# A block-recurrent attention and a serf layer on one core: the first batch's list of steps rewritten, with half of the state loads later

## The chip, the core and the metric

One of the eight cores of a Trainium2 chip runs the whole kernel. The time is the device time of one execution in microseconds (us), and the median of three runs is given. A core has TensorE (PE; its weight loads are PEld in the profile), VectorE (DVE), ScalarE (ACT), GpSimd (POOL) and SyncE (SP). They run side by side, each in the order of its own instructions, and wait for each other by semaphores. SP issues nearly all the DMAs here, and it too works in order: a DMA whose condition is not met holds up all that stand behind it.

## The reference

Inputs are x (8 batches, 8 heads, 512 tokens, 64 wide), state (8, 8, 32, 64), both float32, and the weights w_in (512 x 2048) and w_out (2048 x 512), which come as 64-bit floats and are worked on as float32.

```python
scores = scale * np.matmul(x, state.transpose(0, 1, 3, 2))
scores = scores - scores.max(-1, keepdims=True)
a = np.exp(scores)
a /= a.sum(-1, keepdims=True) + 1e-09
xread = np.matmul(a, state)
# the same with x and state exchanged gives sread; both are joined:
# 8 * (512 + 32) = 4352 rows of 8 heads * 64 = 512 numbers
h = x @ w_in
sp = np.maximum(h, 0.0) + np.log1p(np.exp(-np.abs(h)))   # softplus
g = h * erf(sp)
return (g @ w_out).astype(np.float32)
```

## The kernel before

**Batches.** Batch 0 is computed by a list of named steps written out by hand (`order0`), and batches 1 to 7 by a loop that comes after it (two halves of the hidden width a batch, seven products where a plain scheme needs eight). The 256 state rows come last. The change is in the list and in one load ahead of it. The last 40 steps of the list are open to the loop's order, so list and loop meet without a gap.

**How the list works.** Every step has a name in the table `do`; the names are run through in the order in which they stand, and `in_order` fixes that order on PE, DVE, ACT and SP. Since each step issues on one engine, the list is four queues in one: only the order among the steps of one engine counts. A number ahead of a name (`3*tm1`) sets `leads[0]`, and the step begins with so many matmuls of the identity with itself (`lead`, line 192), which compute nothing that is used. They run as soon as their PSUM buffer is free, ahead of the step's own inputs.

**The steps of batch 0**, with the engine and the line in the profile:

- `x0` to `x3`: PE turns two heads of x each (L780); `x0_v` and so on: the copy out of PSUM. A last letter `_a` puts a copy on ACT (L756) and `_v` on DVE (L757).
- `st`: PE turns the state of batch 0 (L796). `s0`, `s1`: scores of four heads each (L807). `tm0`, `tm1`: the scores turned (L815).
- `max`, `less`, `sum`, `inv`, `norm` on DVE and `exp` on ACT: the softmax over states for either group of heads. `ta0`, `ta1`: its result turned (L826), copied by `ta0_` and `ta1_` into `aT`. `to0`, `to1` hold only fill.
- `m00` to `m32`: PE mixes the state with a part of w_in (L908): first digit the group of 512 hidden columns (0 to 3), second digit the part. `m00x` and `m00y` are halves. `m020_a` and the like are copies. With it xread needs no product of its own: `h01` is `aT` by mixed part (L919), a 128 x 512 block of h of group 0.
- `soft` and `erf` on ACT (L952; L954, or L957 for two blocks), `mul` on DVE (L959). Softplus, erf and exp each need a table that ACT loads before (ACT_TABLE_LOAD).
- `p021`: group 0, output row block 2, hidden block 1: g times w_out (L926), summed in one of four PSUM banks `o0` to `o3`.
- `big`, `wt`, `wz`, `wn`, `tw`, `read`: the other softmax, over tokens, and sread.
- `u0`, `u1`: PE turns the states of batches 1 to 7 (`turn_states`, L893) in the banks `o2` and `o3`, and `u0_v`, `u1_v` copy them back. A `p` step in bank o2 or o3 comes after that.
- `q` (scores), `n0`, `n1` (mixed parts), `qm` to `qr`, `cm`, `ca`: preparation of batch 1. `lxq1..`, `lxq2`, `lx1`: loads of x for batches 1 and 2. `kept` writes w_in to DRAM.

**Weights.** They come as 64-bit words in pieces of 1 MB, i0, i1, o0, o1, i2 and so on (i of w_in, o of w_out; group g uses i(2g), i(2g+1), o(2g), o(2g+1)). `fetch` (a `get` in the list) issues the next piece on SP (L156) into one of three `raw` buffers, and thus waits until DVE and ACT have done with the piece three before. ACT does `i2a0` and `i2a1` (L166, L168) and DVE `i2v0`, `i2v1`, `i2v2` (L171, L172, L173) to make float32 of it. Piece i0 is done in halves (`i0a0`, `i0+a0`).

**Ahead of the list**, SP issues its half of x, the state of batch 0, the pieces i0, i1 and o0, and then `load_st` (L125): eight DMAs, one for each head, of the states of batches 1 to 7.

Of the kernel before, what the change touches and what calls it, by code (L numbers as in the profile page):

```python
# [17 lines left out]
def kernel(  # L18
# [18 lines left out]
    B, H, S, D = x.shape  # L37
# [59 lines left out]
    def load_xq(b, hs=range(H)):  # L97
# [11 lines left out]
    st = const.tile([P, B, P], F32, name="st")  # L109
    away0 = ring[:, 1, 0].rearrange("p k i t -> p (k i t)")  # L110
    st0 = away0[:, 512:640].rearrange("p (g d) -> p g d", g=2)
    x0 = xin.tile([P, NC, H, D], F32, name="x").rearrange("p c h d -> p (c h d)").rearrange(
        "p (h c d) -> p h c d", h=H, c=NC)
# [5 lines left out]
        if i == 1:  # L119
            nc.sync.dma_start(out=st0, in_=state[0].rearrange("(g h) n d -> (h n) g d", g=2))  # L120

    def load_st():
        for h in range(H):
            i, e = h // 2, h % 2
            nc.sync.dma_start(out=st[Ns * i:Ns * i + Ns, 1:B, D * e:D * e + D],  # L125
                              in_=state[1:B, h].rearrange("b n d -> n b d"))
# [571 lines left out]
    def put_x(b, h):  # L698
        rows = out[TB * b:TB * b + S].rearrange("(p c) e -> c p e" if b == 0 else
                                                "(c p) e -> c p e", p=P)  # L700

        def go(r, ot, c=slice(0, d_model), more=False):
            if more:
                nc.gpsimd.dma_start(out=rows[2 * h + r][:, c], in_=ot[:, c], accum_op=ALU.add)  # L704
            else:
                nc.sync.dma_start(out=rows[2 * h + r][:, c], in_=ot[:, c])
        return go
# [35 lines left out]
    def fetch():  # L743
        if len(made) < len(pieces):
            kind, j = w = pieces[len(made)]
            made[w] = (weights_in if kind == "i" else weights_out)(j)
# [4 lines left out]
    def step(name, f, *args):  # L751
        do[name] = lambda: f(*args)

    def copied(name, out, in_):

        do[name + "a"] = lambda: nc.scalar.copy(out(), in_())  # L756
        do[name + "v"] = lambda: nc.vector.tensor_copy(out(), in_())  # L757
# [124 lines left out]
    def groups0():  # L882
# [47 lines left out]
        def put(r):  # L930
            ot = outs.tile([P, d_model], F32, name="ot", bufs=3)
            nc.scalar.copy(ot, acc[r])
            put_x(0, r // 2)(r % 2, ot)

        for k, bs in enumerate((slice(1, 5), slice(5, B))):
            step("u%d" % k, turn_states, k)
            copied("u%d_" % k, lambda bs=bs: st[:, bs, :], lambda k=k: ps_s[k])
# [106 lines left out]

    for _ in range(3):
        fetch()
    load_st()
    start0()
    groups0()
    weights0()  # L1050
    ready = next0()

    order0 = """
        first x0 x0_v x1 x1_a st st_v i0a0 x2 x2_v s0 x3 i0v0 s00_v i0a1 i0v1 i0v2 s01_a tm0 x3_a
        i0+a0 i0+v0 i0+a1 max0 s1 s10_a i0+v1 s11_a less0 exp0 m00x i1a1 3*tm1 i0+v2 max1 m00y
        m000_a sum0 m001_a get 6*to1 m01x less1 m01y exp1 lxq14 inv0 norm0 4*ta0 i1a0 sum1 inv1
        m010_v norm1 u0 o0a0 o0a1 ta1 m011_a ta1_a i1v0 ta0_v h000 i1v1 i1v2 h01 m02 o1a0 o1v0 o0v0
        h001 o1a1 u1 m021_v m020_v soft01 lxq11 o0v1 o0v2 u0_v get soft00 h03 erf00+ h02 soft02
        mul00 p020 p000 p010 u1_v soft03 p030 o1v1 mul01 p011 erf02+ big1 p031 p001 p021 big0 big
        wt1 o1v2 wt0 mul03 mul02 p012 i2a0 wz wn0 tw0 i2a1 p033 i2v0 i2v1 i2v2 get p022 p002 tw0_a  # L1060
        i3a0 i3v0 wn1 m10 m101_v i3a1 i3v1 p013 m100_a get o2a0 h11 i3v2 o2a1 h10 get m12 m121_v
        p023 o2v0 p032 lxq17 p003 soft11 get soft10 erf10+ m120_v h13 h12 o2v1 mul10 o2v2 mul11 o3a0
        o3a1 p110 i4a0 p120 p101 p130 soft13 lxq10 p121 p111 o3v0 o3v1 i4v0 o3v2 i4a1 i4v1 i4v2
        lxq13 soft12 erf12+ get get lxq12 p131 p100 mul13 mul12 i5a0 i5v0 i5a1 p123 m20 p113 m200_a
        p103 m201_a p122 i5v1 get h21 i5v2 m22 h20 o4a0 o4v0 o4a1 o4v1 m220_v o4v2 m221_v tw1 tw1_v
        soft21 h22 h23 lxq15 o5a0 lxq16 get get o5v0 p133 o5a1 p112 p132 o5v1 o5v2 get soft20 erf20
        mul20 soft23 p102 p220 soft22 erf22 xq1v mul22 i6a0 i6v0 erf23 mul23 p230 i6a1 read read_a
        i6v1 i6v2 p210 erf21 mul21 q q1_a qm1 qm3 p203 q0_a qm0 i7a1 qm6 p233 qm2 qm4 n1 n10_a p213
        n11_a i7a0 i7v0 p201 m30 p221 p223 m301_a i7v1 m300_a o6a1 n0 o6a0 n00_v h31 n01_a h30 get
        p200 o7a0 get o6v0 p212 soft31 soft30 p211 qm5 i7v2 m32 cm0 cm1 cm3 erf31 p232 erf30 qm7  # L1070
        o6v1 kept p222 m321_a m320_a h33 p231 lxq2 mul30 o6v2 p300 qm8 mul31 o7v0 o7a1 o7v1 qe0 qs0
        qe2 qe3 qe1 qs1 h32 soft32 erf32 p301 get qs2 qr0 qr2 ca0 soft33 get erf33 qr1 qr3 mul32
        o7v2 p320 ca1 ca3 p311 lx1 p202 p321 cm2 p331 mul33 ca2 p310 p330
    """
    steps0 = order0.split()
    for n, name in enumerate(steps0):
# [246 lines left out]
```

## Time and profile before

| | us |
|---|---|
| three runs | 718.74, 719.79, 720.80; median 719.79 |
| profiled execution | 718.98 |
| its span, from first to last instruction | 717.2 |
| PE busy | 707.9 |
| DVE, ACT busy | 541.1, 377.3 |
| first product of batch 1 on PE (the list's work on PE is over) | 109.18 |

A line of a timeline gives start and duration in us, engine, line of the source, operation, what it writes and reads, how many instructions are merged in it, and in brackets the idle time of the engine before it with what ended that. A line of waits gives who waited for whom, then us in all, how many times, and the longest. `x18` on PE counts two instructions for each float32 matmul. The granted TensorE clock is 1.0 through the span.

### The profile page before, as it was taken

Reading aid. Unit: us, or ns where it says so; the run is one execution under the profiler, and the core shown is the slowest. Engines: PE = TensorE matmul, PEld = TensorE weight load, DVE = VectorE, ACT = ScalarE, POOL = GpSimd, SP = SyncE. Lnnn points to the kernel's source line nnn. Section 1 sums busy time; section 2 is a strip of 40 time slices with the busy share of each in tenths; the row PEclk is TensorE's granted clock in tenths of the full one; section 3 lists DMA queues with packets and bytes.
Section 4 is the critical chain, followed back from the end, with each engine's and each line's share of the span. In section 5 each row is a group of like instructions: output and inputs, shape, how many; then the busy total and the mean of one; then the engine's idle time right before and its main releaser. Section 6 shows DMA issues by size and latency. Waiting matters only on the chain.

```text
span 717.2 us, 10922 instructions
## 1 busy us (share of the span) xinstructions
PE 707.9 (99%) x4273; PEld 560.0 (78%) x4273; DVE 541.1 (75%) x876; ACT 377.3 (53%) x537; POOL 25.2 (4%) x34
## 2 busy tenths in 40 slices
PE   8899999999999999999999999999999999999998
PEld 6344347688878878887888878887888888889997
DVE  5888898889868987798776967697877757664533
ACT  5899895647364525544455435462464535442340
POOL 0000000000100000000000000000000000000000
PEclk9999999999999999999999999999999999999999
DMA  8679786650348162513623280615142321102100
GB/s 268 191 215 276 235 225 189 141 169 30 49 95 211 27 134 46 160 36 92 96 30 146 60 148 1 176 31 149 28 114 75 93 43 24 35 30 30 21 11 29
DMA packets 144067, 74.64 MB, mean 104 GB/s; under 512 B 123024, under 2 KB 132624, under 8 KB 142480
## 3 DMA queue, kind: packets, MB, share of 16 engines
q1 hardware_dynamic: 139152, 65.89, 33.3%
q0 software_dynamic: 4032, 7.34, 7.7%
q8 instruction: 33, 0.54, 0.3%
q10 hardware_dynamic: 832, 0.72, 0.3%
q14 instruction: 18, 0.15, 0.1%
HBM read 49.81 MB, written 20.45 MB: 98 GB/s over the span
## 4 chain that ended last, share of the span: by engine, by line
PE 94%; DMA 3%; ACT 2%; DVE 0%; issue 0%; SPq 0%
PE o L641 48%; PE h L489 13%; PE at L489 10%; PE o L926 6%; PE h L534 3%; PE o L616 3%; DMA raw<-in_moe_w_out_dram 2%; PE h L383 2%; PE at L383 2%; PE h L919 1%; PE at L919 1%; PE at L275 1%; PE o L224 1%; DMA x<-in_x_dram 1%; PE at L908 1%; ACT L957 0%
## 5 line engine op out<-in xcount | busy, mean ns | idle before, releaser
L641 PE MATMUL o<-w_out,ring 128*128 128x256 f32 x896 | 203.0, 379 | 0.0
L641 PEld LDWEIGHTS o<-w_out,ring 128*128 128x128 f32 x896 | 169.9, 190 | 24.9 <-DVE ring L1126 0.8
L641 PE MATMUL o<-raw,ring 128*128 128x256 f32 x672 | 161.4, 381 | 0.0
L641 PEld LDWEIGHTS o<-raw,ring 128*128 128x128 f32 x672 | 126.6, 190 | 25.8 <-ACT m L385 9.2
L482 ACT ACTIVATE ring<-ring 128x512 f32<-128x512 f32 x112 | 70.6, 630 | 59.7 <-DVE ring L472 59.1
L489 PE MATMUL h<-aT,m 128*128 128x256 f32 x336 | 81.9, 379 | 0.0
L1126 DVE TENSOR_TENSOR ring<-ring 128x1024 f32<-128x1024 f32 (+1 forms) x61 | 70.7, 1200 | 4.5 <-ACT ring L546 4.5
L489 PEld LDWEIGHTS h<-aT,m 128*128 128x128 f32 x336 | 63.8, 190 | 10.1 <-issue 1.4
L472 DVE TENSOR_TENSOR ring<-ring,at 128x512 f32<-128x512 f32 x84 | 57.1, 679 | 16.9 <-PE at L489 15.2
L926 PE MATMUL o<-w_out,ring 128*128 128x512 f32 x128 | 59.5, 599 | 0.8 <-DVE ring L959 0.8
L472 DVE TENSOR_TENSOR ring<-ring,h 128x512 f32<-128x512 f32 x56 | 38.0, 678 | 21.6 <-PE h L489 20.4
L626 DVE TENSOR_TENSOR ot<-uv,o 128x256 f32<-128x256 f32 (+1 forms) x56 | 30.9, 552 | 30.5 <-PE o L641 28.2
L664 ACT COPY ot<-o 128x256 f32<-128x256 f32 x28 | 10.4, 372 | 77.9 <-PE o L641 77.9
L704 POOL DMA_DIRECT2D out_dram<-ot x28 | 24.5, 943 | 653.3 <-DVE ot L626 475.4
L926 PEld LDWEIGHTS o<-w_out,ring 128*128 128x128 f32 x128 | 23.5, 190 | 28.3 <-issue 25.3
L626 DVE TENSOR_TENSOR ot<-ot,o 128x256 f32<-128x256 f32 x56 | 22.1, 415 | 27.9 <-ACT ot L664 27.7
L504 ACT COPY ring<-h 128x512 f32<-128x512 f32 x28 | 16.4, 586 | 47.9 <-PE h L489 47.9
L673 DVE TENSOR_TENSOR ring<-ring 128x512 f32<-128x512 f32 x56 | 38.6, 689 | 1.4
L674 DVE TENSOR_TENSOR ring<-ring 128x512 f32<-128x512 f32 x56 | 36.2, 683 | 0.0
L385 ACT COPY m<-h 128x512 f32<-128x512 f32 x13 | 7.6, 586 | 46.3 <-PE h L383 46.1
L546 ACT ACTIVATE ring<-ring 128x2048 f32<-128x2048 f32 x16 | 30.5, 1904 | 0.0
L495 ACT COPY ring<-h 128x512 f32<-128x512 f32 x28 | 16.4, 586 | 24.6 <-PE h L489 24.6
(202 smaller groups left out, 971.3 us busy)
## 6 DMA issues: line engine op xcount, KB each, us to landing
w_in<-kept_in SPq DMA_DIRECT2D x7, 2048.0 KB, 8.7
out_dram<-ot SPq DMA_DIRECT2D x33, 256.0 KB, 2.2
raw<-in_moe_w_in_dram SPq DMA_DIRECT2D x16, 512.0 KB, 5.3
raw<-in_moe_w_out_dram SPq DMA_DIRECT2D x8, 1024.0 KB, 5.2
xq<-in_x_dram SPq DMA_DIRECT2D x112, 64.0 KB, 3.0
x<-in_x_dram SPq DMA_DIRECT2D x56, 128.0 KB, 3.1
out_dram<-ot POOLq DMA_DIRECT2D x28, 256.0 KB, 4.5
sc<-xT SPq DMA_DIRECT2D x112, 32.0 KB, 1.9
```

The costliest lines, as they stand in the source:

```text
L383: nc.tensor.matmul(out=ps[k][e][q, :], lhsT=st[r, b, q], rhs=of_group[g][r, :, i, :], start=True, stop=True)
L472: add = lambda o, x, y: nc.vector.tensor_tensor(o, x, y, op=ALU.add)
L482: nc.scalar.activation(out=s[k], in_=hs[k], func=ACTF.Softplus)
L489: nc.tensor.matmul(out=out[:, i], lhsT=x[:, q:q + P], rhs=y, start=(first and i == 0), stop=(i == 1), skip_group_check=not first)
L546: nc.scalar.activation(out=s, in_=s, func=ACTF.Erf)
L626: add = lambda o, x, y: tt(o, x, y, op=ALU.add)
L641: nc.tensor.matmul(out=out, lhsT=lhs[:, i, :], rhs=rhs[:, g, i, :], start=(start and i == 0), stop=(i == GF - 1), skip_group_check=not start)
L673: return [lambda: tt(S1, A21, A22, op=ALU.add), lambda: tt(S2, S1, A11, op=ALU.subtract), lambda: tt(S3, A11, A21, op=ALU.subtract), lambd ...
L674: lambda: tt(S3, A11, A21, op=ALU.subtract), lambda: tt(S4, A12, S2, op=ALU.subtract)]
L704: nc.gpsimd.dma_start(out=rows[2 * h + r][:, c], in_=ot[:, c], accum_op=ALU.add)
L926: nc.tensor.matmul(out=acc[r], lhsT=gT[g][:, i, P * r:P * r + P], rhs=w_out[:, GF * g + i, :], start=(made_of[r] == 1), stop=(made_of[r] = ...
L1126: nc.vector.tensor_tensor(s[:, ks], s[:, ks], hs[:, ks], op=ALU.mult)
```

## The change

`load_st` now takes a list of heads. It is no longer called ahead of the list but is two steps in it: `lst1` (heads 4 to 7), right after `st`, which on SP comes after o0 and before the `get` of o1; and `lst0` (heads 0 to 3), which on SP comes after that `get`. The steps `u0` and `u1` stand behind `m02` instead of one ahead of `ta1` and one ahead of `h03`. The rest of the list is put in a new order. Ten copies go to the other engine (ACT to DVE: `x1_`, `s01_`, `m011_`, `tw0_`, `m100_`, `m201_`, `read_`; DVE to ACT: `ta0_`, `m020_`, `n00_`). The fill changes from `3*tm1 6*to1 4*ta0`, 13 pieces, to `2*tm0 3*m00y 14*to0 3*ta1`, 22 pieces. Softplus, erf and exp take turns on ACT 22 times instead of 20. All other steps are the same as before.

```diff
-    def load_st():
-        for h in range(H):
+    def load_st(hs):
+        for h in hs:
             i, e = h // 2, h % 2
             nc.sync.dma_start(out=st[Ns * i:Ns * i + Ns, 1:B, D * e:D * e + D],
                               in_=state[1:B, h].rearrange("b n d -> n b d"))
...
+        for k in range(2):
+            step("lst%d" % k, load_st, range(4 * k, 4 * k + 4))
         for k, bs in enumerate((slice(1, 5), slice(5, B))):
             step("u%d" % k, turn_states, k)
...
-    load_st()
     start0()
...
     order0 = """
-        first x0 x0_v x1 x1_a st st_v i0a0 x2 x2_v s0 x3 i0v0 s00_v i0a1 i0v1 i0v2 s01_a tm0 x3_a
-        i0+a0 i0+v0 i0+a1 max0 s1 s10_a i0+v1 s11_a less0 exp0 m00x i1a1 3*tm1 i0+v2 max1 m00y
-        m000_a sum0 m001_a get 6*to1 m01x less1 m01y exp1 lxq14 inv0 norm0 4*ta0 i1a0 sum1 inv1
-        m010_v norm1 u0 o0a0 o0a1 ta1 m011_a ta1_a i1v0 ta0_v h000 i1v1 i1v2 h01 m02 o1a0 o1v0 o0v0
-        h001 o1a1 u1 m021_v m020_v soft01 lxq11 o0v1 o0v2 u0_v get soft00 h03 erf00+ h02 soft02
-        mul00 p020 p000 p010 u1_v soft03 p030 o1v1 mul01 p011 erf02+ big1 p031 p001 p021 big0 big
-        wt1 o1v2 wt0 mul03 mul02 p012 i2a0 wz wn0 tw0 i2a1 p033 i2v0 i2v1 i2v2 get p022 p002 tw0_a
-        i3a0 i3v0 wn1 m10 m101_v i3a1 i3v1 p013 m100_a get o2a0 h11 i3v2 o2a1 h10 get m12 m121_v
...
+        first x0 x0_v x1 x1_v st lst1 st_v x2 x2_v x3 x3_a i0a0 s0 s00_v i0a1 s1 s01_v i0v0 i0v1
+        s10_a s11_a 2*tm0 max0 i0+a1 i0v2 tm1 i0+a0 less0 i0+v0 exp0 3*m00y m001_a max1 i0+v1 m00x
+        sum0 m000_a less1 inv0 i0+v2 i1a0 norm0 14*to0 ta0 get i1a1 exp1 m01y sum1 m01x inv1 norm1
+        3*ta1 o0a0 m011_v ta0_a o0a1 m010_v ta1_a h000 h001 h01 i1v0 i1v1 o0v0 lst0 soft00 i1v2 m02
+        o0v1 m021_v u0 u0_v u1 u1_v lxq16 o1a0 soft01 m020_a h02 o0v2 h03 erf00+ mul01 p001 o1v0
+        p021 mul00 p020 p010 get o1a1 o1v1 o1v2 p011 get p030 big0 p000 soft03 soft02 erf02+ mul02
+        p012 p002 mul03 i2a0 i2v0 get i2a1 p031 p003 p023 big1 big wt1 i2v1 i2v2 wt0 wz m10 wn0 i3a0
+        i3a1 i3v0 p022 p013 m100_v wn1 o2a1 tw0 m101_v h11 lxq17 h10 o2a0 soft11 i3v1 tw0_v i3v2
...
     """
```

More of the change, by code (lines that the diff above doesn't have):

```diff
@@ L1059 @@
-        mul00 p020 p000 p010 u1_v soft03 p030 o1v1 mul01 p011 erf02+ big1 p031 p001 p021 big0 big
-        wt1 o1v2 wt0 mul03 mul02 p012 i2a0 wz wn0 tw0 i2a1 p033 i2v0 i2v1 i2v2 get p022 p002 tw0_a
-        i3a0 i3v0 wn1 m10 m101_v i3a1 i3v1 p013 m100_a get o2a0 h11 i3v2 o2a1 h10 get m12 m121_v
-        p023 o2v0 p032 lxq17 p003 soft11 get soft10 erf10+ m120_v h13 h12 o2v1 mul10 o2v2 mul11 o3a0
-        o3a1 p110 i4a0 p120 p101 p130 soft13 lxq10 p121 p111 o3v0 o3v1 i4v0 o3v2 i4a1 i4v1 i4v2
-        lxq13 soft12 erf12+ get get lxq12 p131 p100 mul13 mul12 i5a0 i5v0 i5a1 p123 m20 p113 m200_a
@@ L1065 @@
[L1065 to L1073, printed above, removed]
+        first x0 x0_v x1 x1_v st lst1 st_v x2 x2_v x3 x3_a i0a0 s0 s00_v i0a1 s1 s01_v i0v0 i0v1
+        s10_a s11_a 2*tm0 max0 i0+a1 i0v2 tm1 i0+a0 less0 i0+v0 exp0 3*m00y m001_a max1 i0+v1 m00x
@@ new lines @@
+        i3a1 i3v0 p022 p013 m100_v wn1 o2a1 tw0 m101_v h11 lxq17 h10 o2a0 soft11 i3v1 tw0_v i3v2
+        o2v0 o2v1 m12 m120_v p033 m121_v get o3a0 p032 h12 o3v0 h13 o2v2 soft10 erf10+ mul10 mul11
+        p120 p130 lxq14 p101 o3a1 o3v1 soft12 p131 p121 get get i4a0 p100 o3v2 i4a1 soft13 i4v0 i4v1
+        i4v2 erf12+ mul12 get p111 lxq13 mul13 p110 p102 m20 i5a0 i5a1 p103 o4a0 m200_a p123 i5v0
+        m201_v i5v1 lxq11 h20 p112 i5v2 m22 o4v0 o4a1 soft20 erf20 m220_v get lxq15 o5a1 lxq10 o5a0
@@ new lines @@
+        h21 soft21 o4v1 m221_v o4v2 p122 tw1 h22 soft22 mul20 p210 lxq12 o5v0 tw1_v p230 o5v1 erf22
+        o5v2 mul22 p220 h23 read erf21 get soft23 mul21 p211 erf23 xq1v mul23 p113 i6a0 p232 read_v
+        p201 i6a1 q i6v0 i6v1 i6v2 get q1_a p231 p200 q0_a qm1 qm3 qm7 get get n1 o6a0 p233 i7a0
+        n10_a n11_a o6v0 cm0 p221 i7a1 i7v0 p212 m30 m300_a p203 m301_a p223 qm0 p202 h31 i7v1 i7v2
+        m32 o6a1 o6v1 o7a1 h30 qm5 soft31 m321_a o7a0 p222 m320_a p133 o6v2 soft30 n0 kept qm2 qm4
@@ L1074 @@
+        qm6 p213 qm8 erf31 mul31 n00_a n01_a erf30 o7v0 cm1 o7v1 qe3 p132 mul30 h33 p301 qe0 qe1 cm2
+        qs0 qe2 qs1 qs2 qr1 h32 qr0 p310 p300 qr2 soft32 qr3 erf32 get ca0 soft33 p311 p330 mul32
+        erf33 lxq2 lx1 o7v2 ca1 ca3 ca2 get get mul33 cm3 p320 p321 p331
     """
```

## The prediction

> **What bounds the kernel now.** I read the page first, then TensorE's waits, then its timeline in the first 45 us. The page's engine rows and the chain by engine:
>
> ```profile
> span 717.2 us, 10922 instructions
> PE 707.9 (99%) x4273; PEld 560.0 (78%) x4273; DVE 541.1 (75%) x876; ACT 377.3 (53%) x537; POOL 25.2 (4%) x34
> PE 94%; DMA 3%; ACT 2%; DVE 0%; issue 0%; SPq 0%
> ```
>
> TensorE (PE) is busy 99% of the span, and the chain runs through it. What is not PE lies at the start. These are PE's waits of the whole span, but for the one before its first instruction:
>
> ```profile
> PE at L815 <- DVE ring L757: 1.4, 1, 1.4
> PE o L926 <- DVE ring L959: 0.8, 1, 0.8
> ...
> PE h L919 <- DVE aT L757: 0.5, 1, 0.5
> PE o L780 <- DMA x<-in_x_dram: 0.5, 1, 0.5
> PE at L908 <- DVE w_in L173: 0.4, 1, 0.4
> PE at L919 <- DVE m L757: 0.4, 1, 0.4
> PE o L893 <- issue: 0.4, 1, 0.4
> PE h L908 <- ACT m L756: 0.4, 1, 0.4
> ```
>
> All end before 41 us; then PE never waits again. Without the one for x, which the diff leaves alone, they sum to 4.6 us with the trace's unrounded values. Beside them PE runs fill: the list's multipliers (`3*tm1`) put identity matmuls ahead of a step. PE's timeline:
>
> ```profile
> 11.33 0.94 PE L192 MATMUL at<-ident 128*128 128x128 f32 x6
> 12.99 1.60 PE L192 MATMUL o<-ident 128*128 128x128 f32 x12
> 15.47 1.16 PE L192 MATMUL o<-ident 128*128 128x128 f32 x8
> 29.37 7.99 PE L926 MATMUL o<-w_out,ring 128*128 128x512 f32 x18 [0.81 <-DVE ring L959]
> ```
>
> Thirteen fills in 3.5 us (from start to next start), so 0.27 each. The real matmuls are the same in both lists, so while PE stays fed afterwards, the change is worth **(waits + fill) before, 4.6 + 3.5 = 8.1 us, less the same sum after**. ScalarE (ACT) has this chain to the second-longest wait, at 29.37:
>
> ```profile
> 16.27 5.31 DMA raw<-in_moe_w_out_dram
> 21.61 1.14 ACT w_out L166
> 22.75 1.07 ACT raw L168
> 23.84 1.28 ACT L952
> 25.14 1.08 ACT ring L952 x2
> 26.24 1.28 ACT L957
> ```
>
> ACT stands in the old list at `o1a0`, the conversion of the second output piece, until that lands at 21.6; only then come softplus, erf and the first `p` step.
>
> **The change part by part.** I wrote both lists out as four columns (PE, ACT, VectorE = DVE, SP), each step with its row's duration, starting when its engine is free and its inputs are ready plus 0.06 us. The old list so written puts `tm0` at 9.7, `m01x` 15.1, `h000` 19.9, `p020` 28.9 and `m10` 40.3; the trace has 9.6, 15.0, 19.6, 29.4, 40.8. I trust it to half a microsecond.
>
> **The fill** grows from 13 to 22 pieces: 22 x 0.27 = 5.9 us, +2.4.
>
> **The start, to `h000`.** x3 is turned before s0, and s0 and s1 are together, so the 1.4 wait before `tm0` is filled by work. In the new columns PE waits 0.2 before s1, 0.1 before `m00y`, then 14 fills (3.8) from 12.3 to 16.1 and 0.5 for `norm0`. DVE has no pause from 8.3 to `norm1` at 18.3 but two of 0.1: these fills lie in time that PE would wait anyway. Only the three before `ta1` cost PE some 0.3. `h000` begins at 19.3 instead of 19.9, with u0 (0.55) still to do: nothing gained here.
>
> **Softplus before `o1a0`.** ACT is free at 20.0 after `ta1_a`. Table load 1.3, `soft00` 0.54, `o1a0` 1.06 (o1 lands at about 21.3, below), `soft01` 0.54, `m020_a` 0.27, table load 1.3 to 1.4, double erf 1.08: 26.2. DVE's `mul01` takes 0.6 and ends, with its tail, at 27.1. PE: `h000` to `h01` 4 x 0.86, `m02` 0.6, u0 and u1 0.97, `h02` and `h03` 3.44: from 19.3 to 27.8. PE comes 0.7 after its input. **The wait of 0.8 at the first `p` goes**, and with it those of 0.5 at `h000` and 0.4 at `h03`.
>
> A rule speaks against this: the Trainium skill (ScalarE: Activation LUTs, What ACT_TABLE_LOAD costs) gives every switch 1283 ns and a drain of 1380, 2.66 us. Two such switches would put `mul01` at 29.7 and give a wait of 1.9; the sum would lose all its gain. The trace has the load at 1.28 and the next ACTIVATE 1.30 after the load began (23.84 to 25.14), so no such drain; I take the row. The new list has 22 loads where the old has 20. The two more (third group, 60 to 75 us) are 2.7 us of ACT, where ACT pauses for 10 us in the old columns and 7 in the new. No cost; without that cover at most 2.7.
>
> **The load of the states.** In the old program SP issues the first output piece (5.01 us), eight st loads, and then the second output piece, o1:
>
> ```profile
> 6.90 9.24 SPq L125 DMA_DIRECT2D st<-in_state_dram  x8
> 16.27 0.39 SPq L156 DMA_DIRECT2D raw<-in_moe_w_out_dram  x1
> SPq L125 <- DMA raw<-in_moe_w_out_dram: 3.3, 1, 3.3
> ```
>
> The eighth waits 3.3 us for an earlier load to land and holds o1 until 16.27. With four ahead that wait is gone, but o1 also needs the buffer of the first piece, whose last reader, `i0+v2`, moves in DVE's column from 13.1 to 15.3 and ends at 15.9. So o1 goes out at 16.0: **0.3 us gained, not 3**. The four late loads are issued behind it at 0.64 each, to 18.5, and land behind its 1 MB. Price: the eight landed from 16.0 (6.90 + 9.1, the longest to landing) to 17.6 (15.8 + 1.8), 0.2 each. o1 at 21.3, the last half at 22.1; PE wants u0 at 23.4, margin 1.3. By the skill (DMA: Bandwidth & Descriptors, Measured) a 64 KB transfer takes 0.95 us: 21.3 + 3.8 = 25.1, and PE, which works in order, would stand 1.8 us at u0 with `h02`, `h03` and every `p` behind it. The sum would be +0.4 us. The row is for these very loads, so I take 0.2. Bounds: 0 to 1.8.
>
> **Weights and copies.** SP's later fetches each wait for a buffer that DVE frees. In the new columns i3 goes out at 26.5 (trace 27.2) and o2 at 30.8 (34.1). `i2v2` ends at 37.4, PE wants `m10` at 38.1: **the 0.4 at `m10` goes**. Ten copies swap between ACT and DVE; by rows of 0.2 to 0.6 DVE gets 1.1 us more. It shows in the end of the DVE column, which moves 0.5 us (108.0 to 107.5) while PE's moves more. At the hand-over the old DVE pauses 1.2 us before its first L472, so up to that DVE may lag without PE seeing it. A loss here is at most PE's gain. SP's block at that place (the copy to DRAM, then 24 loads) waits for `i7v2`, which comes at 86.8 against 89.9 in the old columns: no loss.
>
> **The sum.** After: waits 0.2 + 0.1 + 0.5 = 0.8, fill 5.9, total 6.7. Before 8.1. **-1.4 us.** The profiled execution took 718.98 us (span 717.2 and 1.8 around it), so 717.6; the three runs' median is 0.8 higher, 719.79, so **718.4 us**, 0.2% faster. What a measurement of this kernel can tell from no change is about 0.3%, 2.2 us.
>
> **The rivals.** *No wait left:* if the 0.8 also goes and in-order PE runs smoother between steps, only fill stands against 8.1: -2.2, 717.6. For: DVE's first copies may come sooner. Against: `norm0` hangs on DVE without pause.
>
> *Given back:* the new columns have many margins under 1 us (`m02` and `h02` 0.1, `n1` 0.4), where PE would wait if DVE or ACT slips by a few tenths; or DVE, 19.0 of 20 us busy from 160 to 180 us, keeps its old time. Then 719.8. Against: the old list had such margins (`h22` 0.03, `q` 0.3) and PE waited at none of them.
>
> *Slower, u0 blocked:* the late halves land after 23.4 and PE stands. From 26.9 on (1.4 gained, 2.2 the other way) it decides; with o1 at 21.3 each load would need 1.4 us, or o1 itself late with 1 us each. At 27.5: -1.4 + 4.1 = +2.7, 722.5. For: they are small loads behind a full queue. Against: 0.2 each.
>
> *Does nothing for o1:* this is in my forecast; the gain comes from ACT's order.
>
> **How the numbers follow.** Forecast 0.58, no wait left 0.16, given back 0.15, u0 blocked 0.11. The range reaches from below the second to past the skill's price of the loads (720.2) and the spread of the runs (718.74 to 720.8): 716.9 to 720.9; it leaves out u0 blocked and half a tenth below. The forecast's own range is 717.4 to 719.5. Faster by over 0.3% (under 717.6): half of no wait left and a fifth of the forecast, 0.20. Slower (over 722): u0 blocked and a little of given back, 0.12. The rest, 0.68, is the same.
>
> **What would show it.** In the changed profile: no PE wait at the first L926 and none at L908 near 38; four runs of fill, 5.9 us in all; waits in the first 45 us near 0.8; the first L952 before o1's L166; the first L489 of PE at 107.8 (now 109.2). It is wrong if L893 waits for st, if PE waits anywhere after 45 us, or if the first L489 is early and the span is not.

## The result

Ten runs of the changed kernel have a median of **717.06 us** (716.64 to 717.82), ten of the kernel before 719.29 (718.74 to 720.80): ratio **0.9969**, 95% interval 0.9959 to 0.9979, 2.2 us less. Two repeats, on two chips, gave 0.9975 (0.9965 to 0.9985) and 0.9975 (0.9967 to 0.9984), so 1.8 to 2.2 us. The forecast was 1.4.

The profiled execution of the changed kernel took 717.82 us, the slowest of its ten. Its page, the engine rows and the chain by engine:

```profile
span 716.0 us, 10962 instructions
PE 709.2 (99%) x4291; PEld 562.4 (79%) x4291; DVE 541.9 (76%) x880; ACT 378.9 (53%) x535; POOL 25.2 (4%) x34
PE 97%; DMA 2%; ACT 0%; SPq 0%; DVE 0%; issue 0%
```

PE is busy 1.3 us longer in a span 1.2 us shorter: fill went where waits were. ACT's 2% of the old chain is gone. (From softplus on, the new kernel's step lines have numbers higher by two: softplus is L954, the double erf L959, `mul` L961.) All of PE's waits, in us in all, times, longest (L192's is the one before the first instruction):

```profile
PE o L826 <- DVE ring L848: 1.1, 1, 1.1
PE o L780 <- DMA x<-in_x_dram: 1.0, 1, 1.0
PE o L192 <- PEq L1308: 0.8, 1, 0.8
PE h L919 <- ACT aT L756: 0.4, 1, 0.4
PE h L908 <- DVE w_in L173: 0.2, 1, 0.2
```

No wait is left at the first `p` (L926), at `tm0` (L815) or at `m10` (the L908 into `at`). What remains, beside short ones, is `ta0` behind `norm0`, 1.1 us where the forecast had 0.5. PE's timeline around it:

```profile
12.42 3.39 PE L192 MATMUL o<-ident 128*128 128x128 f32 x28
16.87 0.66 PE L826 MATMUL o<-ident,ring 128*128 128x128 f32 x4 [1.06 <-DVE ring L848]
...
24.15 0.98 PE L893 MATMUL o<-ident,st 128*128 128x128 f32 x7
24.97 3.63 PE L919 MATMUL at<-aT,m 128*128 128x512 f32 x8
28.43 10.46 PE L926 MATMUL o<-w_out,ring 128*128 128x512 f32 x24
```

The long fill, then the one wait; `u0` and `u1` (L893) follow without one. ACT's timeline shows softplus begun before o1's conversion:

```profile
20.75 1.28 ACT L954 ACT_TABLE_LOAD   x1
22.04 0.60 ACT L954 ACTIVATE ring<-h 128x512 f32<-128x512 f32 x1
22.54 1.16 ACT L166 ACTIVATE w_out<-raw 128x1024 f32<-128x1024 f32 x1
23.66 0.60 ACT L954 ACTIVATE ring<-h 128x512 f32<-128x512 f32 x1
```

And SP's shows o1 at 16.30, where the old kernel had 16.27:

```profile
6.79 3.42 SPq L125 DMA_DIRECT2D st<-in_state_dram  x4
16.30 0.38 SPq L156 DMA_DIRECT2D raw<-in_moe_w_out_dram  x1
16.73 1.93 SPq L125 DMA_DIRECT2D st<-in_state_dram  x4
```

### The profile page after: what moved, and what is told of

Read it like the earlier page. It is cut to its first block, busy times and chain, and to the rows that moved or that the text cites. A ratio compares the mean times of both kernels' runs of the same rounds, so it can differ in the third digit from the quotient of the medians.

```text
span 716.0 us, 10962 instructions
## 1 busy us (share of the span) xinstructions
PE 709.2 (99%) x4291; PEld 562.4 (79%) x4291; DVE 541.9 (76%) x880; ACT 378.9 (53%) x535; POOL 25.2 (4%) x34
## 4 chain that ended last, share of the span: by engine, by line
PE 97%; DMA 2%; ACT 0%; SPq 0%; DVE 0%; issue 0%
PE o L641 48%; PE h L489 14%; PE at L489 10%; PE o L926 8%; PE h L534 3%; PE o L616 3%; PE at L919 2%; PE h L919 2%; PE h L383 2%; DMA raw<-in_moe_w_out_dram 2%; PE at L383 2%; PE at L275 1%; PE o L224 1%; DMA x<-in_x_dram 1%; PE at L908 1%; PE at L1018 0%
## 5 line engine op out<-in xcount | busy, mean ns | idle before, releaser
L926 PE MATMUL o<-w_out,ring 128*128 128x512 f32 x128 | 59.5, 599 | 0.0
L926 PEld LDWEIGHTS o<-w_out,ring 128*128 128x128 f32 x128 | 23.7, 190 | 28.1 <-issue 26.6
L504 ACT COPY ring<-h 128x512 f32<-128x512 f32 x28 | 16.4, 586 | 47.9 <-PE h L489 47.9
L489 PE MATMUL at<-sy,sx 128*128 128x256 f32 x112 | 28.7, 379 | 0.0
```

The costliest lines, as they stand in the source:

```text
L489: nc.tensor.matmul(out=out[:, i], lhsT=x[:, q:q + P], rhs=y, start=(first and i == 0), stop=(i == 1), skip_group_check=not first)
L926: nc.tensor.matmul(out=acc[r], lhsT=gT[g][:, i, P * r:P * r + P], rhs=w_out[:, GF * g + i, :], start=(made_of[r] == 1), stop=(made_of[r] = ...
```

## The experiments

Each ratio is to the kernel before on the same chip in the same session. I call two theories *order* (the gain comes from the order of the steps on ACT, DVE and PE) and *loads* (it comes from o1 no longer standing behind eight state loads).

**The changed kernel again**, twice, with nothing edited.

> The changed kernel once more, beside the three others. Both theories expect what was measured first: about 2.2 us less than the kernel before, a ratio of 0.997. If x lands as in the profile of before (TensorE's first turn at 4.7 instead of 5.1 us), the wait before ta0 should be nearer to 0.5 than to 1.06 us.

717.14 against 719.36 us: 0.9975. PE's first turn was at 4.83; `ta0` still waited 1.1:

```profile
PE o L826 <- DVE ring L848: 1.1, 1, 1.1
...
PE at L815 <- ACT ring L756: 0.7, 1, 0.7
```

I had expected a wait nearer to 0.5. So the 1.1 is not from x landing late. It is 1.06 in every profile here with 14 pieces of fill before `ta0`.

> The changed kernel on the same chip and beside the same runs of the kernel before as the old list with more fill: ratio 0.997 to 0.9975, and every run at full clock (none of its 18 so far had a stretch at half clock).

717.42 against 719.29: 0.9975. Every one of its 11 runs had the full clock. The profiled one, 718.32 us, waited longer than the other two profiles of this kernel: 2.6 us after x, of which 0.9 at `ta1`.

**The new order with the old loads.**

```diff
     for _ in range(3):
         fetch()
+    load_st(range(H))
     start0()
...
-    ... st lst1 st_v ... o0v0 lst0 soft00 ...
+    ... st st_v ... o0v0 soft00 ...
```

> The new list with all eight state loads ahead of it, as in the old program. Theory 'order' (the gain comes from the order of the steps on ACT, DVE and PE; the moved loads do nothing): the eighth load again waits for o0 to land, o1 goes out at 16.3 to 18 us and lands at 21.6 to 23, its conversion begins at 22.5, so no new PE wait: ratio 0.997, within 0.3 us of the new kernel. Theory 'loads' (the gain comes from o1 no longer standing behind eight loads): the gain goes, ratio 0.9995 to 1.000.

717.47 us, ratio **0.9977** (0.9968 to 0.9986): the gain stays. SP shows that the old hold-up was back:

```profile
7.08 11.01 SPq L125 DMA_DIRECT2D st<-in_state_dram  x8
18.21 0.39 SPq L156 DMA_DIRECT2D raw<-in_moe_w_out_dram  x1
```

o1 went out 1.9 us later than in the new kernel's profile and landed at 23.3; PE had no wait at L926. The new list has room for an o1 that lands 1.7 us later. *Loads* is out: the gain is there without the split, and with it o1 goes out no sooner than in the old kernel (16.30 against 16.27).

**The old order with the new loads.** Its edit, on the old list:

```diff
-    ... st st_v ... get 6*to1 ... norm1 u0 o0a0 ... h01 m02 o1a0 ... o1a1 u1 m021_v ...
+    ... st lst1 st_v ... get lst0 6*to1 ... norm1 o0a0 ... h01 m02 u0 u1 o1a0 ... o1a1 m021_v ...
```

> The old list with the loads split as in the new one and u0, u1 behind m02. Theory 'loads': the whole gain, ratio 0.997. Theory 'order': in the old list i0+v2 ends at 13.7, so o1 really goes out 2.5 us sooner (13.8) and lands near 19.6; ACT no longer waits for it, but PE's wait at the first L926 falls only from 0.8 to about 0.3, because softplus still stands behind two conversions: -0.5 us, ratio 0.9993.

718.98 us, ratio 0.9998 (0.9989 to 1.0006), against 0.9993 expected from *order* and 0.997 from *loads*. Here o1 did go out 2.2 us sooner, and it bought nothing that can be measured. (The four runs at full clock have 718.78, 0.5 below the old kernel's, as *order* expected; four are too few to tell.) The edit also moves `u0` and `u1`, so their place is not the gain by itself either. SP's timeline:

```profile
6.99 2.89 SPq L125 DMA_DIRECT2D st<-in_state_dram  x4
14.10 0.39 SPq L156 DMA_DIRECT2D raw<-in_moe_w_out_dram  x1
```

PE's waits in the same profile:

```profile
PE at L815 <- DVE ring L757: 1.7, 1, 1.7
...
PE o L926 <- DVE ring L961: 0.4, 1, 0.4
```

The wait at the first `p` falls from 0.8 to 0.4, as forecast to within a tenth; the wait at `tm0` (L815) is that of the old order. This profile also had a stretch of half clock, to which I come below.

**The new list with o1 converted before softplus.**

```diff
-    ... ta1_a h000 ... lxq16 o1a0 soft01 ... get o1a1 o1v1 ...
+    ... ta1_a o1a0 o1a1 h000 ... lxq16 soft01 ... get o1v1 ...
```

> The new list with one thing undone: o1a0 and o1a1 stand before soft00 on ACT again, as in the old list. Theory 'order': ACT stands idle until o1 lands at 21.6, soft00 begins near 25 instead of 22.0, and PE waits about 1.9 us at h02 or at the first L926: 1.9 us slower than the new kernel, ratio to before 0.9996. Theory 'loads': o1 lands as before, nothing lost, ratio 0.997.

719.24 us, ratio **1.0005** (0.9996 to 1.0014): one pair of ACT steps put back, and the whole gain is gone, 2.1 us against the changed kernel beside it. ACT's timeline:

```profile
21.11 1.18 ACT L166 ACTIVATE w_out<-raw 128x1024 f32<-128x1024 f32 x1 [1.13 <-DMA raw<-in_moe_w_out_dram]
22.19 1.17 ACT L168 ACTIVATE raw<-raw 128x1024 uint32<-128x1024 uint32 x1
...
24.67 1.09 ACT L954 ACTIVATE ring<-h 128x512 f32<-128x512 f32 x2
```

and PE's:

```profile
26.08 3.70 PE L919 MATMUL at<-aT,m 128*128 128x512 f32 x8 [1.69 <-ACT m L756]
```

Softplus begins at 24.67 instead of 22.04, the `m020` copy comes behind it, and PE waits 1.7 us for that copy. It doesn't follow that this pair alone is the gain: in the new list everything else is packed so that this wait is not covered by another.

**The new list without fill.** All multipliers are taken out of the list; the identity matmuls of the 22 pieces are gone, nothing that is computed changes.

> The new list without any fill (no identity matmuls; the steps are the same). Theory 'fill lies in waiting time': PE idles where the fill was, waits of about 6.5 us in all, of which 4.3 before ta0, and the time is that of the new kernel or 0.2 us less: ratio 0.9975 within 0.0005. Rival 'the fill holds the clock': a record of the run with the old list and split loads has a stretch of 3.4 us at half clock (12.0 to 15.4 us). If the idle 4.3 us bring such a stretch while real matmuls run, up to 3.4 us of work take twice their time: up to 1.7 us more, ratio up to 1.000.

718.24 us, ratio 0.9996 (0.9987 to 1.0004): by the ratios, fill that computes nothing is worth 1.5 us. Busy time by stretch, before, in and after the stretch of half clock (PEclk is the granted clock, third value from the end):

```profile
5.00:12.00 7.00, 6.01 (x105) 4.40 (x110) 5.56 (x11) 3.50 (x7) 0.00 (x0) 1.00 1.05 352
12.80:23.00 10.20, 6.18 (x29) 3.33 (x30) 9.96 (x19) 7.58 (x11) 0.00 (x0) 0.50 0.80 212
23.00:30.00 7.00, 7.00 (x37) 3.25 (x36) 5.14 (x8) 6.73 (x8) 0.00 (x0) 1.00 0.53 159
```

and PE's timeline before and in it:

```profile
11.86 0.45 PE L908 MATMUL h<-w_in,ring 64*32 64x128 f32 x16 [0.91 <-DVE w_in L173]
16.79 1.08 PE L826 MATMUL o<-ident,ring 128*128 128x128 f32 x4 [4.48 <-DVE ring L848]
...
19.42 5.39 PE L919 MATMUL h<-aT,m 128*128 128x512 f32 x8
```

The wait before `ta0` is 4.48 us, 4.3 expected; but from 12.8 to 23.0 us the clock is half, and the eight matmuls of `h00` and `h01` take 5.39 us, where a profile at full clock (the repeat) has 3.69. The rival was right and my theory of idle fill wrong.

**Without the three pieces before `ta1` only** (`3*ta1` becomes `ta1`).

> The new list without the three pieces of fill before ta1. By the forecast they cost PE some 0.3 us, of which the columns give back only 0.1 because m02 then waits for i1v2: 0.1 to 0.3 us less than the new kernel, not to be told from it.

718.37 us, ratio 0.9991 (0.998 to 1.0002). Five of 12 runs had a mean granted clock of 0.995 to 0.997, which is what some 4 to 7 us at half clock make of 717. The other seven have a median of 717.69, no less than the changed kernel's 717.06 to 717.42 in its three sessions, so taking out the fill that I had charged with 0.3 us gained nothing. The profile is one of the five. Its waits, and the stretch of half clock:

```profile
PE o L826 <- DVE ring L848: 1.8, 2, 1.1
...
PE h L919 <- ACT aT L756: 0.5, 1, 0.5
```

```profile
19.40:26.10 6.70, 6.16 (x8) 2.47 (x8) 4.49 (x5) 5.09 (x7) 0.00 (x0) 0.50 0.78 211
```

**lst0 behind the next weight piece.** `lst0` moves from ahead of `soft00` to behind a `get` put after `i1v2`; the later `get` goes.

```diff
-    ... o0v0 lst0 soft00 i1v2 m02 ... p010 get o1a1 ...
+    ... o0v0 soft00 i1v2 get lst0 m02 ... p010 o1a1 ...
```

> The new list with lst0 later: behind the get of i2, which itself stands where DVE is done with i1. The four loads go out at 24 to 26 us and land behind 1 MB more, near 28.5 to 29.5. Rival 'u0 blocked' (PE works in order and stands at u0 with all later steps behind it): PE waits 4 to 5.6 us at u0 where it now comes at 24.2, and the time is 4 to 5.6 us longer than the new kernel's: ratio to before 1.003 to 1.0055. If instead the states don't matter before batch 1, the ratio stays 0.9975.

726.76 us, ratio **1.0109** (1.0096 to 1.0122), 7.8 us over the kernel before and, by the ratios, some 9.6 over the new one, where 4 to 5.6 had been expected. PE's timeline:

```profile
30.20 1.73 PE L893 MATMUL o<-ident,st 128*128 128x128 f32 x7 [5.89 <-DMA xq<-in_x_dram]
31.71 5.34 PE L919 MATMUL at<-aT,m 128*128 128x512 f32 x8
```

and the busy time by engine in the stretch that follows the wait, the granted clock third from the end:

```profile
28.40:35.20 6.80, 5.00 (x12) 2.97 (x13) 3.88 (x6) 0.97 (x1) 0.00 (x0) 0.50 0.16 22
```

PE stood 5.9 us at `u0` (the row names a later DMA; the last state load landed at 29.95), and the wait brought 6.8 us of half clock, in which `h02` and `h03` took 5.3 instead of 3.7 us. The states do matter here, and this wait cost its own 5.9 us and about 2.5 more, half of the 5.0 us of work at half clock (30.20 to 35.21).

**Small moves on ACT and DVE, 17 pieces of fill**, an attempt at a version better than both.

> The new list with its first 85 steps moved a little on ACT and DVE (x1, x2 and m010 copies on ACT, i0+v2 and the o0 and o1 pieces shifted by a place or two) and 17 pieces of fill: in the columns PE is free 0.4 to 0.5 us sooner. Ratio to before 0.997; if DVE stays the bound of the start without change, 0.9975, which can't be told apart by much.

717.48 us, ratio 0.9988 (0.9977 to 0.9999). Not better: four of 12 runs had lost clock; its profile (one of the four) shows `h00` and `h01` at

```profile
20.51 6.41 PE L919 MATMUL h<-aT,m 128*128 128x512 f32 x8 [0.90 <-ACT aT L756]
```

The eight runs at full clock have 717.21. I found no version that beats the changed kernel.

**The old list with more fill**: `5*tm0` and `7*to1` for `tm0` and `6*to1`.

> The old list, all steps and loads as they were, with six more pieces of fill where PE waits: five before tm0 (1.2 us of its wait of 1.4) and one before m01x. Theory 'order': fill in waiting time only keeps the clock; runs with a stretch at half clock, nearly half of the old kernel's runs so far, become few, and the median falls by 0.1 to 0.3 us to that of the old kernel's full-clock runs: ratio 0.9997. Rival 'the fill is the gain': the old list with more fill comes near the new one, ratio 0.9975.

720.02 us, ratio 1.0011 (0.9999 to 1.0023), where *order* had 0.9997 and the rival 0.9975. Ten of 11 runs were at full clock, where 7 of 21 of the old kernel beside it were not, but the time did not fall: fill by itself is not the gain. Its profile has waits of PE that the profile of the old kernel had at less than half this length:

```profile
PE o L893 <- DMA st<-in_state_dram: 1.3, 1, 1.3
PE at L919 <- DVE m L757: 1.2, 1, 1.2
```

In this execution o0 landed at 17.35 us instead of 15.81 and the eighth state load at 19.16 instead of 17.6, and `u0`, which the old list has ahead of `ta1`, stood for them. Its first turn of x also took 1.94 us instead of 1.07: the record of full clock begins at 6.71 us here and at 3.73 in the old kernel's profile. Why the median is no lower than the old kernel's, one profile doesn't show. Three of its runs are above 721.

The mean granted clock of all timed runs, by kernel (it leaves out the first microseconds, before a record begins):

| kernel | pieces of fill | runs with mean clock under 0.999 | median of the others, us |
|---|---|---|---|
| before (three sessions) | 13 | 35 of 80 | 719.31, 718.88, 719.25 |
| changed (three sessions) | 22 | 0 of 29 | 717.06, 717.14, 717.42 |
| new order, old loads | 22 | 0 of 11 | 717.47 |
| new list, o1 before softplus | 22 | 3 of 11 | 719.18 |
| old list, new loads | 13 | 7 of 11 | 718.78 |
| old list, more fill | 19 | 1 of 11 | 719.88 |
| new list, without 3 before `ta1` | 19 | 5 of 12 | 717.69 |
| new list, small moves | 17 | 4 of 12 | 717.21 |
| late loads (`lst0` behind i2) | 22 | 4 of 4 | none |
| new list without fill | 0 | 11 of 11 | none |

Side by side, the old and the changed kernel differ by 2.2 and 1.8 us at full clock too, so the gain is not the clock's; but no run of the changed kernel lost any, and near half of the old one's did.

## Why the prediction was right, and where it was not

**Direction and size.** 717.06 lies in the range, close to its lower end (716.9). The sign was right and the size 1.4 instead of 1.8 to 2.2; the first measurement stands just past the bound of 0.3%, to which 0.20 was given, the two repeats just inside it. 717.06 is below the forecast's own range (717.4 to 719.5), at the rival *no wait left* (0.16); 0.5 of the distance to 718.4 is that the old kernel came out at 719.29 and not at 719.79. That the sum came so near is in part luck, as the table below shows. The prediction's sums hold to 0.1 us (25.1 less 23.4 is 1.7, not 1.8).

**Softplus before `o1a0`: right.** The wait at the first `p` is gone, and putting the pair back costs 2.1 us with a wait of 1.7 (1.9 expected). ACT's table load took 1.28 and the next ACTIVATE began 1.29 after it began, so the row held and not the 2.66 of the page that the prediction cites.

**The loads: right.** o1 went out at 16.30 (16.0 forecast), not 3 us sooner. The four late loads landed 0.4 us apart, neither 0.2 nor the 0.95 of the cited page (whose row is for transfers issued by GpSimd), behind o1 at 21.6; the last at 23.06, 1.1 us before `u0` (margin 1.3 forecast). Either split of the loads on either list moved the time by no more than the measurement tells.

**`m10`: right.** o2 was issued at 31.38 (30.8 forecast) and PE had no wait.

**The start: mis-sized.** Waits after x came to 1.8 us in the first profile, 1.9 in the repeat and 2.6 in the second repeat, not 0.8. In the first profile `norm0` ended 0.3 us later than in my columns, and 14 pieces of fill took 3.39 us, 0.24 each instead of 0.27, so PE stood longer in front of `ta0`. Fill in all was 5.6 instead of 5.9.

**The step that failed: "the real matmuls are the same in both lists".** They are the same in number but not in time. From start to next start, without waits and fill, the steps from x to the first `p` took 16.97 us in the old profile and 15.68 in the repeat of the new one. The mixed parts (L908) went from 1.82 to 1.36; 0.3 of that is at `m00x` and `m00y`, between which the old list has fill and `tm1`, while the new one runs them together. Turns (L780, L826, L893) and the hidden blocks (L919) save 1.0 together, most of it where the old list had a wait behind them. `h02` and `h03`, the same eight matmuls everywhere, took 3.67 us in the two profiles with a wait of 0.8 behind them, 3.60 in the one with 0.4, and 3.46 to 3.54 in the eight at full clock with none. I read that as the last matmul of a step running to its end before a wait, in time that counts as busy; no run tests it by itself, and the ends of matmuls are modelled in the profile. So the sum at full clock, from the turn of x0 to the first product of batch 1 (104.47 us before, 102.39 in the repeat):

| us | forecast | measured |
|---|---|---|
| waits | -3.8 | -2.7 |
| fill | +2.4 | +2.1 |
| the steps before the first `p` | 0 | -1.3 |
| the steps after it | 0 | -0.2 |
| sum | -1.4 | -2.1 |

Two errors stood against each other: waits and fill saved 0.8 us less than forecast, the steps 1.5 more. These are single executions. The first profile gives -2.0; the second repeat only -0.9, with its waits of 2.6 us and a first turn of x that lay in part before the record of full clock.

**Fill "in time that PE would wait anyway": half right.** It costs nothing that showed where it stands, but I left out what it does: without it the clock drops, and 1.5 us are lost. And taking out the pieces charged with 0.3 at `ta1` gained nothing.

**The rivals.** *No wait left* came to the right time by another way: waits remained, the steps were shorter. *Given back* did not happen: PE had no wait after 21 us in the first profile and was 1.6 us ahead at the first product of batch 1 (107.6 us, 107.8 forecast). From there to PE's end the repeat took 604.7 us, the old kernel 604.6; the first profile lost 0.4, most of it in the reads (L275). *u0 blocked* did not happen in the new kernel, but it was a true danger, and its price was set too low by the clock.

**What stays open.** How much of the gain over many runs is the old list's exposure to late landings: o0 landed at 15.81 us in the first profile of the old kernel and at 16.5 to 18.5 in all others here. The old list with more fill shows `u0` standing for that in one execution; the old kernel itself was profiled only once. How the gain divides among softplus, the order of the first turns and mixed parts, the ten copies and `m10` is read from the profiles: only softplus was put back by itself, and fill taken out.

## What to carry over

Where PE is full, a start is worth its waits and its fill, but count a wait as longer than its idle time: here the steps around the waits took longer too (16.97 us in the old list, 15.68 in the new one), in part because steps that could run together were parted. Before a load is moved, look for the second condition of what it holds up: in the new list a buffer held o1 until 16.30, as long as the queue had in the old one, and in the old list, where the split let o1 go 2.2 us sooner, nothing measurable came of it. Fill that computes nothing can't be judged by the wait that it covers alone: add up all of PE's idle time within 3.4 us, and look at the granted clock over many runs.

## What the runs showed of the hardware

The granted clock falls to half in stretches of 3.41, 6.83 or 10.24 us, multiples of one length. So I divided each of the twelve profiles, up to PE's end, into stretches of 3.41 us from its first record of full clock and added up PE's idle time in each. At full clock, no stretch with 1.35 us or less had half clock behind it, and both with 1.85 or more did. Those with 1.35 and more, by idle time:

| profile | stretch, us | PE idle in it, us | clock behind it |
|---|---|---|---|
| old list, more fill | 16.95 to 20.37 | 1.35 | full |
| new list, small moves | 15.77 to 19.18 | 1.43 | half |
| before | 7.15 to 10.56 | 1.44 | full |
| new list without fill | 9.38 to 12.79 | 1.48 | half |
| old list, new loads | 8.56 to 11.97 | 1.49 | half |
| new list, o1 before softplus | 24.59 to 28.00 | 1.49 | full |
| changed, second repeat | 15.70 to 19.11 | 1.51 | full |
| new list, without 3 before `ta1` | 15.93 to 19.34 | 1.85 | half |
| late loads | 24.97 to 28.39 | 3.41 | half |

Several short waits in one such stretch, 1.4 to 1.5 us in sum, were thus enough in some executions and not in others, and where the stretches begin differs from run to run (3.58 to 6.71 us), so that runs of one kernel differ. In all five profiles the full clock came back behind a stretch without any idle time. The Trainium skill (TensorE: Matmul & The Clock Gate, What's actually happening) gives a free-running window of 3413 ns and a gate that an idle window closes. The lengths agree, and so does the profile with the late loads; the rest doesn't: without fill, the half clock began at 12.79 us, 0.5 us into the wait of 4.48, where a wholly idle window would have ended only at 16.20. At half clock the eight 128x512 matmuls of `h00` and `h01` took 5.4 to 6.7 us instead of 3.7.
